# Keeping TensorE's instructions of the first layer in written order behind the opening as well

## The chip, the cores and the metric

The kernel runs on one core of one Trainium2 chip. The metric is the device time of one execution in microseconds, from launch to the last output, as the median of three runs. A profile of one further execution gives the times of the single instructions. Five engines matter: TensorE (PE, matrix products, with its own weight loads PEld), VectorE (DVE), ScalarE (ACT), GpSimd (POOL), and SyncE (SP), which here only issues DMA transfers. Each engine takes its instructions strictly in the order in which they stand in its own stream; a semaphore holds an instruction until the work that it reads is done, and everything behind it on that engine is held too.

## What is computed

A retention layer (attention with a fixed decay and no softmax) over 4 batches, 8 heads, 576 positions and head size 64, and behind it two feed-forward layers over the 2304 tokens, 512 wide with a hidden width of 2048:

```python
scores = scale * np.matmul(q, k.transpose(0, 1, 3, 2))
Dmat = np.where(rel >= 0, gamma[:, None, None] ** rel[None, :, :], 0.0)
x = np.matmul(scores * Dmat[None], v)         # then (B*S, H*D)
h = x @ w_in;  g = h * np.cos(h);  y = g @ w_out            # first layer
h = y @ w_in;  g = where(h >= 1, h, where(h <= -1, 0, (h + 1) ** 2 / 4));  out = g @ w_out   # second layer
```

Inputs and weights are given in float32 (the feed-forward weights in a wider form that the kernel converts itself).

## The kernel before

Every operand of a matrix product is split in a high and a low part, and a product is made of three: high by high, low by high and high by low.

**The first layer** runs in slots. The tokens are cut in five blocks (256, then four of 512), the hidden width in 16 pieces; a slot is one piece of one block, 80 in all. Slots 0 to 31 interleave blocks 0 and 1, slots 32 to 47 are block 2, 48 to 63 block 3, 64 to 79 block 4. In a slot, TensorE makes the *first product* (`mm1`, 12 matmuls into a PSUM bank `h`, line 599). Then follows a chain over three engines: a rounded copy on ACT (`turns`, 647), the remainder on DVE (`rounded`, 651), sine and square on ACT (655, 656), times h on DVE (660), the high part `gh` on ACT (667) and the low part `gl` on POOL (672). In blocks 0 and 1 ACT first copies h out of PSUM (`hs`, 642). TensorE's *second product* (`mm2`, 12 matmuls, lines 614 to 616) reads `gh`, `gl` and a piece of `w_out` and adds into four PSUM banks `bky` (two, `bkS` and `bkO`, for the 256-wide block). It is written two slots behind its first product: the text of slot s issues `mm1(s)`, then the rest of the chain of s-1, then `mm2(s-2)`.

**Retention** of the tokens of block 3 is done while block 2's slots run, that of block 4 while block 3's run: nine chunks of up to 128 tokens, here numbered 1 to 9 (1 to 5 belong to block 3). A chunk visits TensorE twice with small 64-row matmuls into the banks `bkS` and `bkO` (line 372). The *scores* visit (`scores`, `across`) comes first. DVE then multiplies both banks by a mask into the tile `R` (`masked`, two instructions on line 460), and the *attend* visit (`attend`, `state`) reads `R`. ACT and DVE then empty the banks into the next block's input (500, 507) and DVE updates a running state `T` (406). Before the chunk POOL scales its q and k (358, 368). The places of these steps are written as half slots: scores at g, attend a third of the way to the chunk's end e.

Beside this, DVE and ACT convert weights in the background (lines 196 to 277), and **the second layer**, from about 459 us on, runs with a scheme of seven products (`hq`, `wq`).

**What sets the order.** All engines' instructions are written in one program text. A scheduler then orders each engine's stream by its own estimate of when things are ready, except where the text pins them. The variable `by_hand` says what is pinned, through a wrapper `Ordered` around each engine; a pinned instruction is kept behind whatever stands before it on its engine. The opening (up to slot 7 or so) is listed by hand and pinned on all engines (`by_hand` 1). Behind it (`by_hand` 2) instructions only stay behind the opening's last one. From slot 24 on nothing is pinned (`by_hand` 0), and in the second layer TensorE alone is pinned (`by_hand` 3). Pinned instructions show line 107, the wrapper's, in place of their own. Line numbers are the same in both kernels. `keep_in_program_order` adds no wait: it fixes only which instruction stands behind which.

Of the kernel before, what the change touches and what calls it, by code (L numbers as in the profile page):

```python
# [89 lines left out]
def retention_moe_kernel(ctx: ExitStack, tc: tile.TileContext, qk, kv, win1, wout1, win2, wout2, rtab, ktab, out):  # L90
    nc = tc.nc
    by_hand = [0]
# [68 lines left out]
    def load_raw(L, i, c, late=False, homes=None):  # L161
        src = wsrc[L, i][c]
        twice = L == 0 and (i, c) not in ONCE
        tag = "raw" if twice else ("raw", "rsh")[turn[0] % 2] if L == 0 else ("raw", "raw", "rsh")[turn[0] % 3]
        turn[0] += not twice and not late
        pool, first, second = (wp, "wo0", None) if late else (cv, tag, "rsh") if homes is None else (wp, *homes)
        t = pool.tile([P, DM, 2], I32, tag=first, name="raw")
        i0 = SY.dma_start(out=t, in_=src)
        if L == 1 and len(done) > 1 and not late:
            behind(i0, done[-2])  # L170
        t2 = None
        if twice:
            t2 = pool.tile([P, 4 * DM], I16, tag=second, name="rsh")
            SY.dma_start(out=t2[:, 1:], in_=src.rearrange("p n two -> p (n two)").bitcast(I16)[:, :4 * DM - 1])
        raws[L, i, c] = t, t2
# [49 lines left out]
    def begin(L, i, c, after=None, late=False):  # L225
        return Conversion(L, i, c, after, late).X()
# [3 lines left out]
    def home1(i, c):  # L230
        if i == 0:
            wi[0, c] = wr.tile([P, 2, DM], F32R, tag="wi", name="wi")
            return wi[0, c]
        wo[0, c] = wp.tile([P, 2, DM], F32R, tag=f"wo{c}", name=f"wo{c}")
        return wo[0, c]

    def store1(c):
        SY.dma_start(out=wd[0, 0, c], in_=f(wi[0, c]))
# [42 lines left out]
    def load_wi(c):  # L281
        t = wr.tile([P, 2, DM], F32R, tag="wi", name="wi")
        SY.dma_start(out=f(t), in_=wd[0, 0, c])
        wi[0, c] = t
# [339 lines left out]
    def evac(s):  # L624
        l, c = slots[s]
        if c != NC - 1:
            return
        o, n = BLOCKS[l]
        per = 512 // n
        for e, y in enumerate(yb.pop(l)):  # L630
            t = stp.tile([P, 512], F32, tag="st", name="st")
            copy_out(e, t, y, -TWOPI)
            SY.dma_start(out=yd[:, e * per:(e + 1) * per, o:o + n], in_=t.rearrange("p (k n) -> p k n", k=per))
# [50 lines left out]
    def steps_of(s, which):  # L684
        for x in which:
            if (x, s) not in taken:
                taken.add((x, s))
                STEPS[x](s)
# [124 lines left out]
    def run_plan(pos):  # L813
        for fn in plan.pop(pos, []):
            fn()
# [173 lines left out]
    def spill_2(i, c):  # L989
        (spill_wi2, spill_wo2)[i](c, begun2.pop((i, c)))  # L990
        if i == 0 and c >= NQ:
            spill_sums(c - NQ)
# [12 lines left out]
    def run_pre(t):  # L1005
        for fn in pre.pop(t, []):
            fn()

    for s in range(N1):
        l, c = slots[s]  # L1010
        if s == 24:
            by_hand[0] = 0
        run_plan(2 * s)
        steps_of(s, "m")
        if s >= 1:
            steps_of(s - 1, "CgG")
        steps_of(s, "haA")

        todo = [x for x in jobs.get(s, []) if x not in opened]
        begun = [begin(0, *x) for x in todo]  # L1020
        for x in todo:
            begun.pop(0).rest(home1(*x))
            if x[0] == 0:
                store1(x[1])
            if queue:
                load_raw(0, *queue.pop(0))
        run_plan(2 * s + 1)
        if s >= LAG:
            steps_of(s - LAG, "M")
            evac(s - LAG)  # L1030
        for x in bgpos.get(s - 2, []):
            spill_2(*x)
        for x in bgpos.get(s, []):
            load_raw(1, *x)
        steps_of(s, "b")
        for x in bgpos.get(s - 1, []):
            begun2[x] = begin(1, *x, after=mark[0])
        for c2 in reload.get(s, []):
            load_wi(c2)

        q = 2 * (s - N1)
        if q >= -22:
            run_pre(q)
            run_pre(q + 1)
# [119 lines left out]
```

## Time and profile before

| | |
|---|---|
| median of 3 runs | 848.73 us (847.38 to 849.69) |
| the profiled execution | 848.21 us |
| its span, first to last instruction | 846.4 us |
| granted TensorE clock over the span | 0.999 of 2.4 GHz |
| PE busy | 835.2 us, 99% of the span |
| DVE, ACT, POOL busy | 576.6, 445.6, 142.2 us |

The span is what the trace covers; 1.8 us of the execution lie around it. A matmul's duration holds its pipeline: a 512-wide one is shown with 389 ns, while the next one starts 227 ns behind it. So a PE that is shown busy can still have been held for a tenth of a microsecond or so, and distances are best read from start to start.

### The profile page before, as it was taken

The numbers are of one execution on the slowest core, as the hardware profiler recorded it, in microseconds if no ns is written. First come the engines' busy times: TensorE is split into PE (matmuls) and PEld (weight loads), VectorE is DVE, ScalarE is ACT, GpSimd is POOL, SyncE is SP. The second block draws the span as 40 slices with busy tenths as digits, with TensorE's granted clock in tenths as the row PEclk, the third lists the DMA queues.
The fourth block names the chain that finished last, engine by engine and source line by source line (L and its number), as shares of the span: only waits on it lengthen the run. The fifth ranks groups of instructions, "written<-read, shape, count | busy, mean of one in ns | idle before, by whom it ended". The sixth has DMA issues, their size and how long they took to land.

```text
span 846.4 us, 14195 instructions
## 1 busy us (share of the span) xinstructions
PE 835.2 (99%) x5279; PEld 717.2 (85%) x5283; DVE 576.6 (68%) x1080; ACT 445.6 (53%) x868; POOL 142.2 (17%) x116
## 2 busy tenths in 40 slices
PE   8999999999999999999999999999999999999998
PEld 5778888888778888888888988989898898898986
DVE  7877888549776889677883676766554766554554
ACT  4877878755555655556665443344333344333333
POOL 3422322432324242222223000000000000000000
PEclk9999999999999999999999999999999999999999
DMA  9987999846868778678867877865755756755532
GB/s 351 407 323 266 340 328 328 308 139 217 286 217 307 275 286 275 228 256 310 298 237 239 276 254 231 273 195 174 258 190 169 275 177 178 261 183 175 160 88 75
DMA packets 68245, 207.72 MB, mean 245 GB/s; under 512 B 7376, under 2 KB 11216, under 8 KB 68176
## 3 DMA queue, kind: packets, MB, share of 16 engines
q1 hardware_dynamic: 68176, 206.81, 71.4%
q8 instruction: 42, 0.69, 0.3%
q14 instruction: 27, 0.22, 0.1%
HBM read 165.89 MB, written 40.89 MB: 244 GB/s over the span
## 4 chain that ended last, share of the span: by engine, by line
PE 86%; DMA 6%; DVE 4%; ACT 2%; issue 1%; SPq 0%; ACTq 0%; DVEq 0%
PE hq L107 20%; PE bky L107 17%; PE h L599 15%; PE bky L614 6%; PE bky L615 6%; PE bky L616 6%; PE bkO L107 4%; PE bkS L107 4%; DMA qkv<-in_kv_dram 2%; PE h L107 2%; PE bkS L372 1%; PE bkO L599 1%; PE bkS L599 1%; PE bkO L372 1%; DVE t L107 1%; DMA rsh<-in_wout_dram 1%
## 5 line engine op out<-in xcount | busy, mean ns | idle before, releaser
L107 PE MATMUL hq<-xc,wq 128*128 128x384 f32 x1008 | 202.8, 336 | 0.0
L107 PEld LDWEIGHTS hq<-xc,wq 128*128 128x128 f32 x1008 | 180.7, 188 | 15.0
L599 PE MATMUL h<-xhl,wi 128*128 128x512 f32 (+1 forms) x576 | 138.7, 388 | 0.0
L599 PEld LDWEIGHTS h<-xhl,wi 128*128 128x128 f32 x576 | 105.8, 188 | 22.6 <-issue 0.7
L107 PE MATMUL bky<-wo,gh 128*128 128x512 f32 x384 | 119.5, 392 | 0.0
L672 POOL TENSOR_TENSOR gl<-t,gh 128x512 fp32r<-128x512 f32 (+1 forms) x57 | 78.1, 1370 | 197.7 <-ACT gh L667 146.2
L781 ACT ACTIVATE t<-t,half 128x384 f32<-128x384 f32 x96 | 58.7, 612 | 86.2 <-DVE t L780 86.1
L614 PE MATMUL bky<-gh,wo 128*128 128x512 f32 x208 | 81.7, 393 | 0.0
L677 ACT ACTIVATE gh<-t 128x384 fp32r<-128x384 f32 x96 | 50.3, 525 | 59.3 <-DVE t L782 59.3
L615 PE MATMUL bky<-gh,wo 128*128 128x512 f32 x208 | 81.1, 390 | 0.0
L616 PE MATMUL bky<-gl,wo 128*128 128x512 f32 x208 | 78.7, 389 | 0.0
L107 PEld LDWEIGHTS bky<-wo,gh 128*128 128x128 f32 x384 | 70.4, 188 | 7.1
L107 PE MATMUL bky<-wo,gl 128*128 128x512 f32 x192 | 76.3, 397 | 0.0
L782 DVE TENSOR_TENSOR t<-t,sC 128x384 f32<-128x384 f32 x96 | 53.3, 555 | 18.9 <-ACT t L781 18.7
L678 DVE TENSOR_TENSOR gl<-t,gh 128x384 fp32r<-128x384 f32 x96 | 53.2, 554 | 18.1 <-ACT gh L677 17.8
L780 DVE TENSOR_SCALAR t<-sC 128x384 f32<-128x384 f32 x96 | 34.3, 358 | 43.4 <-ACT sC L767 41.7
L667 ACT ACTIVATE gh<-t 128x512 fp32r<-128x512 f32 (+1 forms) x57 | 35.3, 619 | 44.1 <-DVE t L660 44.1
L655 ACT ACTIVATE t<-t 128x512 f32<-128x512 f32 (+1 forms) x56 | 35.0, 624 | 40.2 <-DVE t L651 40.1
L107 PE MATMUL h<-xhl,wi 128*128 128x256 f32 (+1 forms) x288 | 52.0, 330 | 0.0
L107 PEld LDWEIGHTS h<-xhl,wi 128*128 128x128 f32 x288 | 43.6, 190 | 5.7 <-issue 0.5
L651 DVE SCALAR_TENSOR_TENSOR t<-t,h 128x512 f32<-128x512 f32 x40 | 27.4, 684 | 30.3 <-ACT t L647 29.8
L767 ACT ACTIVATE sC<-hq 128x384 f32<-128x384 f32 x24 | 11.8, 490 | 67.1 <-PE hq L107 67.1
(188 smaller groups left out, 1480.8 us busy)
## 6 DMA issues: line engine op xcount, KB each, us to landing
wq<-wq SPq DMA_DIRECT2D x72, 512.0 KB, 3.9
wi<-wd SPq DMA_DIRECT2D x48, 512.0 KB, 4.9
wo<-wd SPq DMA_DIRECT2D x48, 512.0 KB, 3.8
raw<-in_win_dram SPq DMA_DIRECT2D x32, 512.0 KB, 6.3
raw<-in_wout_dram SPq DMA_DIRECT2D x32, 512.0 KB, 5.7
qkv<-in_qk_dram SPq DMA_DIRECT2D x16, 512.0 KB, 6.1
qkv<-in_kv_dram SPq DMA_DIRECT2D x16, 512.0 KB, 7.0
wd<-wi SPq DMA_DIRECT2D x16, 512.0 KB, 6.1
```

Source lines behind the costliest of these rows:

```text
L107: ins = fn(*args, **kw)
L599: lastpe[0] = PE.matmul(hp[s][:, :n], w[:, a, kb, :], x[b][:, kb, :], start=(i == 0), stop=(i == 3 * KB - 1))
L614: PE.matmul(o, w[:, 0, es], a, start=first and e % per == 0, stop=False, skip_group_check=True)
L615: PE.matmul(o, w[:, 1, es], a, start=False, stop=False, skip_group_check=True)
L616: PE.matmul(o, w[:, 0, es], b, start=False, stop=last, skip_group_check=True)
L655: A.activation(u, u, AF.Sin, scale=TWOPI / 2)
L667: A.activation(gh[s], rt[s], AF.Copy)
L672: G.tensor_tensor(out=gl[s], in0=u, in1=f(gh[s]), op=ALU.subtract)
L677: A.activation(a, u, AF.Copy)
L678: V.tensor_tensor(out=b, in0=u, in1=f(a), op=ALU.subtract)
L781: A.activation(t, t, AF.Square, scale=0.5, bias=half)
L782: V.tensor_tensor(out=t, in0=t, in1=h, op=ALU.max)
```

## The change

One number: from slot 24 to the end of the first layer, `by_hand` is 3 where it was 0, so TensorE's stream there keeps the order of the text. The other engines stay free; the scheduler orders them anew around the pinned TensorE.

```diff
     for s in range(N1):
         l, c = slots[s]
         if s == 24:
-            by_hand[0] = 0
+            by_hand[0] = 3
         run_plan(2 * s)
         steps_of(s, "m")
```

Up to slot 23 all streams are the same. TensorE, at slot 24, before: `h` is a first product, `bky` a second product, and `wo_1611` the weights of the second product of slot 21, `wo_1820` those of slot 20.

```order
L107 MATMUL bkO<-gl,wo_1820 128x256
L107 MATMUL h<-xhl,wi 128x256 x8
L599 MATMUL h<-xhl,wi 128x512 x12
L107 MATMUL bky_1009<-gh,wo_1611 128x512 x2
L107 MATMUL bky_1010<-gh,wo_1611 128x512 x2
```

And now:

```order
L107 MATMUL bkO<-gl,wo_1820 128x256
L107 MATMUL h<-xhl,wi 128x256 x8
L107 MATMUL bky_1009<-gh,wo_1611 128x512 x2
L107 MATMUL bky_1010<-gh,wo_1611 128x512 x2
L107 MATMUL bky_1011<-gh,wo_1611 128x512 x2
L107 MATMUL bky_1012<-gh,wo_1611 128x512 x2
L107 MATMUL bky_1009<-gl,wo_1611 128x512
L107 MATMUL bky_1010<-gl,wo_1611 128x512
L107 MATMUL bky_1011<-gl,wo_1611 128x512
L107 MATMUL bky_1012<-gl,wo_1611 128x512
L107 MATMUL h<-xhl,wi 128x512 x12
```

The first product of slot 24 (the row with 12 matmuls of 512) stood ahead of slot 21's second product and stands behind it now.

TensorE, at the sixth chunk, before: the end of block 2's last second product (`wo_2161`, slot 47), then the start of the attend visit, which reads `R`.

```order
L614 MATMUL bky_2528<-gh,wo_2161 128x512
L615 MATMUL bky_2528<-gh,wo_2161 128x512
L616 MATMUL bky_2528<-gl,wo_2161 128x512
L599 MATMUL h<-xhl,wi 128x512 x5
L372 MATMUL bkS<-R,qkv 64x128
L372 MATMUL bkO<-R,qkv 64x128
```

And now, from the end of the scores visit (`qkv,T`) to the attend visit:

```order
L107 MATMUL bkO<-qkv,T 64x128
L107 MATMUL bkS<-qkv,T 64x128
L107 MATMUL h<-xhl,wi 128x512 x12
L107 MATMUL bkS<-R,qkv 64x128
L107 MATMUL bkO<-R,qkv 64x128
```

Between the scores and the attend visit stood the first product of slot 49, the second of slot 47 and 5 matmuls of the next first product; now the first product of slot 49 alone stands there. Chunks 1, 2, 3, 4, 5 and 8 likewise have one product block between the two visits now, chunks 7 and 9 two. The scores visit of chunk 6 was cut in two before, with 2 of its matmuls ahead of the first product of slot 46, and is whole now.

DVE, behind the second chunk, before: `T` is its state update, `xhl` its low part, `t` the chains of the slots (651 is `rounded`, 660 times h), and `cw`, `W`, `X`, `C` the conversions.

```order
L209 TENSOR_SCALAR W<-X 128x512
L210 TENSOR_SCALAR X<-W 128x512
L406 SCALAR_TENSOR_TENSOR T<-T,ktb,bkS 128x64 x2
L406 SCALAR_TENSOR_TENSOR T<-T,ktb,bkO 128x64 x2
L216 SCALAR_TENSOR_TENSOR cw<-C,X 128x512
L660 SCALAR_TENSOR_TENSOR t<-t,h 128x512
L507 TENSOR_TENSOR xhl<-bkS,xhl 128x2x128
```

And now:

```order
L406 SCALAR_TENSOR_TENSOR T<-T,ktb,bkS 128x64 x2
L406 SCALAR_TENSOR_TENSOR T<-T,ktb,bkO 128x64 x2
L277 TENSOR_TENSOR tw<-V,tw 128x4x256
L507 TENSOR_TENSOR xhl<-bkS,xhl 128x2x128
L507 TENSOR_TENSOR xhl<-bkO,xhl 128x2x128
L204 TENSOR_SCALAR C<-raw 128x512
L205 SCALAR_TENSOR_TENSOR C<-raw,C 128x512
L651 SCALAR_TENSOR_TENSOR t<-t,h 128x512
L209 TENSOR_SCALAR W<-X 128x512
L210 TENSOR_SCALAR X<-W 128x512
L216 SCALAR_TENSOR_TENSOR cw<-C,X 128x512
L660 SCALAR_TENSOR_TENSOR t<-t,h 128x512
```

The state update, the low part and a conversion step moved ahead of slot 36's `rounded`.

## Rows read from the trace of the kernel before

**Rows 1.** Stretches of the span: us, busy time of each engine, PEclk, DMA share, GB/s.

```profile
160.00:350.00 190.00, 190.00 (x1586) 153.70 (x1585) 139.79 (x246) 109.77 (x200) 61.94 (x47) 1.00 0.72 250
...
459.00:834.00 375.00, 374.56 (x1862) 336.04 (x1861) 224.50 (x451) 145.46 (x267) 1.29 (x1) 1.00 0.63 202
```

**Rows 2.** Timeline of PE at slot 24: start us, us, engine, line, operation, tiles.

```profile
133.90 1.12 PE L107 MATMUL h<-xhl,wi 128*128 128x256 f32 x8
134.99 3.02 PE L599 MATMUL h<-xhl,wi 128*128 128x512 f32 x12
137.85 1.98 PE L107 MATMUL bky<-gh,wo 128*128 128x512 f32 x8
...
140.92 0.28 PE L614 MATMUL bkS<-gh,wo 128*128 128x256 f32 x1
...
142.36 1.24 PE L599 MATMUL h<-xhl,wi 128*128 128x256 f32 x9
```

**Rows 3.** Timeline of ACT and of POOL there, slots 21 and 24.

```profile
135.91 0.62 ACT L107 ACTIVATE gh<-t 128x512 fp32r<-128x512 f32 x1
141.06 0.59 ACT L642 ACTIVATE hs<-h 128x512 f32<-128x512 f32 x1
136.66 1.30 POOL L107 TENSOR_TENSOR gl<-t,gh 128x512 fp32r<-128x512 f32 x1 [4.25 <-ACT gh L107]
147.41 1.31 POOL L672 TENSOR_TENSOR gl<-t,gh 128x512 fp32r<-128x512 f32 x1 [4.38 <-ACT gh L667]
```

**Rows 4.** Timeline of PE around the sixth chunk.

```profile
268.19 2.88 PE L599 MATMUL h<-xhl,wi 128*128 128x512 f32 x12
270.91 0.39 PE L614 MATMUL bky<-gh,wo 128*128 128x512 f32 x1
...
283.06 0.39 PE L614 MATMUL bky<-gh,wo 128*128 128x512 f32 x1
```

**Rows 5.** Timeline of DVE before the sixth chunk's attend visit.

```profile
271.80 0.69 DVE L651 SCALAR_TENSOR_TENSOR t<-t,h 128x512 f32<-128x512 f32 x1 [2.70 <-ACT t L647]
272.41 1.31 DVE L209 TENSOR_SCALAR W<-X 128x512 int32<-128x512 int32 x1
...
281.20 0.41 DVE L209 TENSOR_SCALAR W<-X 128x512 int32<-128x512 int32 x1
...
284.79 0.55 DVE L460 TENSOR_TENSOR R<-bkS,mtb 128x384 f32<-128x384 f32 x1
```

**Rows 6.** Timeline of POOL in the same stretch.

```profile
272.13 1.30 POOL L358 TENSOR_TENSOR qkv<-qkv,qtb 128x512 f32<-128x512 f32 x1 [0.95 <-DMA qkv<-in_qk_dram]
```

**Rows 7.** Timelines of DVE and PE at the eighth chunk.

```profile
324.89 0.54 DVE L460 TENSOR_TENSOR R<-bkS,mtb 128x384 f32<-128x384 f32 x1
324.50 2.88 PE L599 MATMUL h<-xhl,wi 128*128 128x512 f32 x12
```

**Rows 8.** Timelines of DVE and PE at the second and the third chunk.

```profile
192.06 1.16 DVE L209 TENSOR_SCALAR W<-X 128x512 int32<-128x512 int32 x1
200.22 0.55 DVE L460 TENSOR_TENSOR R<-bkS,mtb 128x384 f32<-128x384 f32 x1
200.00 2.88 PE L599 MATMUL h<-xhl,wi 128*128 128x512 f32 x12
215.71 0.55 DVE L460 TENSOR_TENSOR R<-bkS,mtb 128x384 f32<-128x384 f32 x1
216.65 0.39 PE L614 MATMUL bky<-gh,wo 128*128 128x512 f32 x1
```

**Rows 9.** Groups of DVE, 165 to 350 us: shapes, count | busy us, mean ns | idle before.

```profile
L507 DVE TENSOR_TENSOR xhl<-bkS,xhl 128x256 fp32r<-128x256 f32 (+1 forms) x8 | 3.1, 391 | 5.2 <-ACT xhl L500 5.0
...
L406 DVE SCALAR_TENSOR_TENSOR T<-T,ktb,bkS 128x64 f32<-128x64 f32 x12 | 2.8, 276 | 0.5 <-PE bkS L372 0.5
```

**Rows 10.** Timelines of DVE and PE at the first chunk.

```profile
181.10 0.55 DVE L460 TENSOR_TENSOR R<-bkS,mtb 128x384 f32<-128x384 f32 x1
183.37 0.39 PE L614 MATMUL bky<-gh,wo 128*128 128x512 f32 x1
```

## The prediction

> **What bounds the kernel now.** I read the busy time by stretches first. In the main part of the stretch that the change reaches, TensorE is busy without a gap (190.00 of 190 us), at a granted clock of 1.00, the upper level of 2.4 GHz [rows 1]. Since a matmul's row also covers its pipeline, that alone proves little. So I went to TensorE's timeline and read from start to start: a product block of twelve 512-wide matmuls takes 270.91 - 268.19 = 2.72 us [rows 4], which is 227 ns a matmul, and a first product behind narrower matmuls 137.85 - 134.99 = 2.86 us [rows 2]. Blocks follow each other at these prices through all of slots 24 to 79. The first layer behind the opening is therefore bound by TensorE's issue, and the order of before already hides every chain on the other engines. Of the second layer's stretch 374.56 of 375 us are busy too [rows 1].
>
> From this follows the form of the sum. The change neither adds nor removes a matmul, so the blocks cost the same in any order. Little can be won. What can be lost is a place where the written order asks for an operand earlier than its engine delivers it: TensorE then stands still, and since it is the bound, all of that goes on the end. So I looked, place by place, for what the new order asks for and when the trace of before had it. All times are put on the clock of the trace of before.
>
> **Slot 24.** Slot 21's second product now follows directly on the matmuls of 133.90, that is at 134.99 [rows 2]. Its high part `gh` is made by ACT from 135.91 to 136.53 [rows 3]. All streams are the same up to there, so nothing makes it earlier. Before, the first product of slot 24 filled that time. TensorE stands still 136.53 - 134.99 = 1.54, with some 0.06 for the signal **1.6 us**. The low part ends at 137.96 and is wanted behind eight matmuls, at 138.4: no second wait.
>
> **Slot 24's own chain.** The 256-wide blocks around it are short (142.36 - 140.92 = 1.44 us [rows 2]), so the written distance of two slots is short here. The first product of slot 24 now ends at 136.6 + 2.72 + 2.86 = 142.2. Behind it come the second product of 22, first of 25, second of 23 (1.44 each) and the first of 26 (2.86): its own second product starts at 149.4, and its third matmul, the first with `gl`, at 149.8. The chain in before, from ACT's copy to the end of POOL's `gl`, ran from 141.06 to 148.72, 7.7 us [rows 3]. Now ACT can start the copy at 142.7 or so, behind a conversion, so `gl` comes at 150.4 to 150.6: a wait of **0.8 us**. From below it is 0 (a chain shorter by 0.8, since ACT and DVE are put in another order there), from above 1.5 (a second conversion in front of the copy).
>
> **Chunks.** The attend visit waits for DVE's second mask instruction. In before a scores visit was followed by two blocks or more; now often by one. So I compare the end of that instruction with the time at which the first block behind the scores visit ended.
> - Chunk 1: ready at 181.65, wanted at 183.37 [rows 10]. No wait, 1.7 us to spare. Chunks 4 and 5 have 64 columns, shorter masks, and no wait either; 7 and 9 keep two blocks.
> - Chunk 2: ready at 200.77, wanted at 200.00 [rows 8], a wait of 0.8 as it stands. But the DVE queue in front of it was late because a conversion step took 1.16 us [rows 8], while the same step takes 0.41 undisturbed [rows 5], with POOL scaling the next chunk's q and k beside it. That next chunk's load waits until the first chunk's attend visit has freed its buffer; that visit now comes one block sooner, so the scaling should be over before the conversion. I take **0.2**, between 0 and 0.85.
> - Chunk 3: ready at 216.26, wanted at 216.65 [rows 8], 0.4 to spare. But DVE now does the state update, the low part and a conversion step ahead of slot 36's `rounded`. Of the six instructions, the four of the update take some 0.23 each (2.8 us for 12) and the two of the low part some 0.39 [rows 9], 1.7 us together; ACT's part of slot 37 stands behind the late slot 36. I take **0.3**, between 0 and 1.2.
> - Chunk 6: ready at 285.34 [rows 5], wanted at 283.06 [rows 4], a wait of **2.3 us**. DVE is busy from 271.80 to there without a break, and what starts it is slot 47's first product, which stands at the same distance as before: from 270.91 to 283.06 stand three blocks, the scores visit and one more block in either order. From below 0.7 (rivals), from above 2.8.
> - Chunk 8: ready at 325.43, wanted at 324.50 [rows 7]. **0.9**, between 0.2 and 1.1.
>
> At chunk 6 the trace shows a conversion step of 1.31 us, begun at 272.41, where the same step took 0.41 at 281.20 [rows 5], and POOL scaling a chunk from 272.13 to 273.43 [rows 6]. The Trainium skill (SBUF — State Buffer, Who interferes with whom) says that DVE's faster mode and GpSimd share a pair of ports under a lock, and that the later one is held until the first has finished. By that rule the step was held until 273.43 and then took its 0.41, so it should have lasted 1.4 us; the trace agrees with 1.31. By that rule the wait at chunk 6 goes down where POOL's scaling no longer falls on these steps; that is the first rival.
>
> **What is given back.** The scores visit of chunk 6 is whole again. A product block behind narrower matmuls costs 2.86 in place of 2.72 [rows 2, 4], 0.14 more; the turn into the narrow ones I put at about as much, so one turn in and out less gives **-0.3 us**, between -0.6 and 0. The second layer is as bound by TensorE as the first [rows 1] and its order is unchanged, so the waits are not made up there.
>
> **Sum:** 1.6 + 0.8 + 0.2 + 0.3 + 2.3 + 0.9 - 0.3 = 5.8 us. The profiled execution took 848.21 (span 846.4 and 1.8 around it), so 854.0. The median of the runs is 0.5 above the profiled execution and within their spread of 2.3; I predict **854.0 us**, slower by 0.7%.
>
> **Rivals.**
> 1. *The DVE backlog dissolves.* With the two waits of slot 24 and earlier attend visits, transfers, and so POOL's scaling, fall on other DVE instructions. At chunk 6 the conversion step would then take 0.41 in place of 1.31, 0.9 less; I put what the steps behind it lose to the rest of the scaling at another 0.7, so the wait falls to 0.7. At chunk 8 it falls to 0.2, chunks 2 and 3 have none. For it: loads are tied to the attend visits. Against it: chunk 7's load, whose scaling falls on chunk 6's backlog, hangs on TensorE's slots as much as on the fifth chunk. Sum 1.6 + 0.8 + 0.7 + 0.2 - 0.3 = 3.0, so 851.2: still slower, by 0.35%.
> 2. *Not slower: the reordered ACT and DVE deliver in time.* The scheduler knows the pinned order and has reordered the other engines for it. If slot 24's own chain and all masks come in time, only the wait for slot 21's `gh` is left, since the streams in front of it are the same: 1.6 - 0.3 = +1.3, 849.5, within 0.3%. It decides from the point on which the masks come one block behind the scores. For it: the mask of chunk 1 had 1.7 us to spare. Against it: DVE's order around the masks of chunks 6 and 8 is unchanged.
> 3. *Late chains feed each other.* Every place at its upper bound: 1.6 + 1.5 + 0.85 + 1.2 + 2.8 + 1.1 = 9.1, 857.3. For it: DVE has little slack (139.79 busy of 190 [rows 1]), and ACT, DVE and POOL also hold later slots back. Against it: a still TensorE gives the others time to catch up.
> 4. *The change does nothing.* Excluded: the streams differ at the places shown.
>
> **How the numbers follow.** The forecast 0.50, rival 1 0.20, rival 2 0.13, rival 3 0.13, and 0.04 for a gain that I don't see, at most the few tenths of the turns between wide and narrow. A measurement of this kernel can tell about 0.3%, 2.5 us. Slower by more than that are the forecast, rival 3, and most of rival 1: 0.80. Within it are rival 2 and the rest of rival 1: 0.17. Faster: 0.03. The range runs from rival 2's 849.5 to 858.5, rival 3 with a microsecond for waits in block 4's slots that I haven't priced; the forecast's own range is 852 to 856.
>
> **What would show it.** In the new profile TensorE should stand still at about 135 us, waiting for ACT's `gh`, for some 1.5 us; at about 151 for POOL's `gl`; and before the attend visits of chunks 6 and 8, waiting for DVE's `R` (about 285 and 330 us). PE's idle time between 134 and 350 us should add up to 5 to 6 us, or a little less where the pipeline hides its first tenths. Blocks between the waits should still take 2.72 us and the second layer its 375. Wrong is the working if a wait of over a microsecond stands at a place not named, if the second layer's length changes, if the granted clock falls behind a wait, or if the masks of chunks 6 and 8 are ready in time.

## The result and the profile after

The changed kernel takes 854.62 us (median of 6 runs, 853.95 to 856.33), the kernel before 848.39 beside it: a ratio of 1.0077 (95% interval 1.0064 to 1.0090), slower, with 854.0 predicted. Timed a second time (the ninth experiment) the ratio was 1.0065 (1.0051 to 1.0079).

The waits of TensorE in the new profile, from 130 us to the second layer (engine, tile, line <- what it waited for: us in total, times, longest). The same view of before had no line.

```profile
PE bkS L107 <- DVE R L460: 2.6, 2, 1.8
PE bky L107 <- POOL gl L672: 1.0, 2, 0.6
PE bky L107 <- ACT gh L107: 0.9, 1, 0.9
```

The stretches that answer to [rows 1] (us, busy time of each engine, PEclk, DMA share, GB/s), before and behind the first layer's end:

```profile
134.00:160.00 26.00, 24.53 (x144) 21.34 (x143) 19.52 (x35) 20.78 (x45) 6.84 (x7) 1.00 0.87 316
160.00:350.00 190.00, 187.38 (x1543) 152.00 (x1542) 135.55 (x245) 108.73 (x196) 60.13 (x47) 1.00 0.71 245
...
465.00:840.00 375.00, 374.55 (x1861) 335.63 (x1860) 224.25 (x451) 144.77 (x267) 1.30 (x1) 1.00 0.62 202
```

TensorE, busy without a gap before, now has holes of 1.47 and 2.62 us, 4.1 together (5.6 in the second profile), where 5 to 6 was predicted; the clock is 1.00 in them and behind them. In 375 us of the second layer TensorE is busy for as long as before.

**Slot 24** [rows 2, 3]. TensorE, ACT's high part of slot 21, and POOL's low part of slot 24, in that order (start, duration, operation, and in brackets the idle time before it and what ended it):

```profile
135.12 1.12 PE L107 MATMUL h<-xhl,wi 128*128 128x256 f32 x8
137.13 2.14 PE L107 MATMUL bky<-gh,wo 128*128 128x512 f32 x8 [0.89 <-ACT gh L107]
...
149.80 0.62 PE L107 MATMUL bky<-gh,wo 128*128 128x512 f32 x2
151.01 0.50 PE L107 MATMUL bky<-gl,wo 128*128 128x512 f32 x1 [0.58 <-POOL gl L672]
...
136.46 0.61 ACT L107 ACTIVATE gh<-t 128x512 fp32r<-128x512 f32 x1
...
149.67 1.28 POOL L672 TENSOR_TENSOR gl<-t,gh 128x512 fp32r<-128x512 f32 x1 [6.75 <-ACT gh L667]
```

Slot 21's second product starts 2.01 us behind the eight narrow matmuls, which last 0.96 undisturbed (in the second experiment): 1.05 lost. Slot 24's second product runs from 149.80 to 153.40, 3.60 in place of 2.72: 0.88 lost. Both waits are the predicted ones. The first is shorter than 1.6 here because this execution's opening was late; of that below.

**Chunk 6** [rows 4 to 6]. TensorE behind the scores visit, DVE up to the masks, and POOL:

```profile
282.49 3.02 PE L107 MATMUL h<-xhl,wi 128*128 128x512 f32 x12
287.27 0.32 PE L107 MATMUL bkS<-R,qkv 64*64 64x128 f32 x1 [1.77 <-DVE R L460]
...
276.80 1.19 DVE L251 TENSOR_TENSOR V<-W,X 128x512 f32<-128x512 f32 x1
278.03 1.15 DVE L270 TENSOR_TENSOR V<-V 128x256 f32<-128x256 f32 x1
279.10 1.51 DVE L263 TENSOR_TENSOR cw<-V,cw 128x256 fp32r<-128x256 f32 x1
...
286.20 0.55 DVE L460 TENSOR_TENSOR R<-bkO,mtb 128x384 f32<-128x384 f32 x1
286.67 0.55 DVE L460 TENSOR_TENSOR R<-bkS,mtb 128x384 f32<-128x384 f32 x1
...
275.99 1.46 POOL L358 TENSOR_TENSOR qkv<-qkv,qtb 128x512 f32<-128x512 f32 x1 [2.04 <-DMA qkv<-in_qk_dram]
277.65 1.24 POOL L368 TENSOR_TENSOR qkv<-qkv,ktb 128x512 f32<-128x512 f32 x1 [0.21 <-DMA qkv<-in_kv_dram]
278.86 1.48 POOL L672 TENSOR_TENSOR gl<-t,gh 128x512 fp32r<-128x512 f32 x1
```

One product block stands between scores and attend, 4.78 us long in place of 2.86: 1.92 lost. The masks are ready at 287.22. In front of them three conversion steps last 1.19, 1.15 and 1.51 while POOL works on chunk 7 and a low part.

**Chunk 8** [rows 7], from the second product behind the scores visit to the attend visit:

```profile
325.74 0.73 PE L107 MATMUL bky<-gh,wo 128*128 128x512 f32 x2
...
329.61 0.32 PE L107 MATMUL bkS<-R,qkv 64*64 64x128 f32 x1 [0.85 <-DVE R L460]
```

The block takes 3.87 us. A second product behind narrow matmuls takes 2.85 to 2.88 undisturbed (behind chunk 6's attend visit, in the two profiles of the change), so 1.0 is lost to DVE's `R`.

**Slot 75**, in block 4, was not named in the prediction. First TensorE and POOL after, then the same before:

```profile
448.06 2.88 PE L107 MATMUL bkS<-xhl,wi 128*128 128x512 f32 x12
450.78 0.61 PE L107 MATMUL bky<-gh,wo 128*128 128x512 f32 x2
451.78 0.50 PE L107 MATMUL bky<-gl,wo 128*128 128x512 f32 x1 [0.38 <-POOL gl L672]
...
450.44 1.29 POOL L672 TENSOR_TENSOR gl<-t,gh 128x512 fp32r<-128x512 f32 x1 [5.13 <-ACT gh L667]
```

```profile
445.79 1.07 PE L599 MATMUL h<-xhl,wi 128*128 128x512 f32 x4
446.70 0.39 PE L614 MATMUL bky<-gh,wo 128*128 128x512 f32 x1
...
448.06 0.84 PE L616 MATMUL bky<-gl,wo 128*128 128x512 f32 x3
...
445.43 1.29 POOL L672 TENSOR_TENSOR gl<-t,gh 128x512 fp32r<-128x512 f32 x1 [5.13 <-ACT gh L667]
```

Before, the scheduler had put four matmuls of the next first product and six of `gh` ahead of the first that needs `gl`. In written order `gl` is wanted third and comes too late, which costs 0.7 us.

**Where the time went.** Each stage below ends where the same amount of matmul work is left before the second layer, so the columns compare the same work; two executions of each kernel.

| stage, us | before | before, again | after | after, again |
|---|---|---|---|---|
| start of the eight narrow matmuls at slot 24 | 133.90 | 132.53 | 135.12 | 133.00 |
| from there to about slot 30's second product | 42.97 | 42.98 | 44.63 | 46.90 |
| chunks 1 to 5 | 83.92 | 83.92 | 83.91 | 83.91 |
| up to chunk 6's scores visit | 15.56 | 15.56 | 14.96 | 14.96 |
| chunk 6 | 15.72 | 15.72 | 17.55 | 17.56 |
| chunks 7, 8 | 41.67 | 41.70 | 42.56 | 42.11 |
| chunk 9, slots to 74 | 107.75 | 107.74 | 107.75 | 107.75 |
| slot 75 | 6.12 | 6.12 | 6.79 | 6.92 |
| to the second layer | 11.78 | 11.79 | 11.81 | 11.81 |
| from the narrow matmuls to the second layer | 325.49 | 325.53 | 329.96 | 331.92 |

In these rows the kernel before repeats to 0.05 us; the change costs 4.5 us in its first profile and 6.4 in the second. The second layer, behind the last row, does not repeat as well: from its first matmul to the end of the span it takes 387.0 and 387.5 us before, 387.4 and 386.4 after. TensorE waits there once for DVE's `gl`, 0.4 to 0.5 us in three of these profiles and not in the fourth. This differs by execution and not by kernel, and the rows leave it out.

**The opening** ends at another time in each execution. In the change's first profile TensorE stood still for 2.1 us at 56 us (for a mask that stands in DVE's queue behind a conversion, whose transfer DVE had waited 5.0 us for), and behind it the granted clock fell (stretches as above):

```profile
56.00:58.00 2.00, 0.00 (x0) 0.00 (x0) 1.66 (x4) 0.58 (x3) 0.00 (x0) 1.00 1.01 399
58.00:60.00 2.00, 1.98 (x17) 1.57 (x18) 1.93 (x6) 1.84 (x6) 0.73 (x1) 0.67 1.02 414
60.00:62.00 2.00, 2.00 (x6) 1.60 (x5) 2.00 (x5) 1.31 (x4) 0.08 (x1) 0.50 0.54 221
62.00:64.00 2.00, 2.00 (x10) 1.57 (x10) 1.97 (x6) 1.97 (x5) 0.00 (x0) 0.98 0.03 12
```

0.50 is the lower level, 1.2 GHz. All instructions up to there are the same in every kernel of this study, so this isn't the change's doing. The table starts behind the opening, because its end (the table's first row) differs by up to 2.6 us between these four profiles.

### The profile page after: what moved, and what is told of

Its sections match the earlier page's. It is cut to its first block, busy times and chain, and to the rows that moved or that the text cites. A ratio compares the mean times of both kernels' runs of the same rounds, so it can differ in the third digit from the quotient of the medians.

```text
span 852.5 us, 14188 instructions
## 1 busy us (share of the span) xinstructions
PE 835.9 (98%) x5279; PEld 717.7 (84%) x5283; DVE 574.1 (67%) x1080; ACT 446.9 (52%) x868; POOL 139.4 (16%) x116
## 4 chain that ended last, share of the span: by engine, by line
PE 69%; DVE 9%; DMA 2%; ACT 2%; issue 1%; SPq 0%; ACTq 0%; DVEq 0%
PE bky L107 27%; PE hq L107 20%; PE h L107 12%; PE bkS L107 5%; PE bkO L107 5%; DVE cw L263 1%; DVE t L651 1%; DVE xc L730 1%; DMA rsh<-in_wout_dram 1%; DMA q<-yd 1%; DMA wq<-cw 1%; DVE t L660 1%; DVE X L250 1%; DVE W L209 0%; DVE V L251 0%
## 5 line engine op out<-in xcount | busy, mean ns | idle before, releaser
L107 PE MATMUL h<-xhl,wi 128*128 128x512 f32 (+1 forms) x864 | 190.4, 369 | 0.0
L107 PE MATMUL bky<-gh,wo 128*128 128x512 f32 x512 | 156.6, 392 | 0.9 <-ACT gh L107 0.9
L107 PEld LDWEIGHTS bky<-gh,wo 128*128 128x128 f32 x512 | 94.9, 188 | 20.9 <-ACT gh L107 1.1
L107 PE MATMUL bky<-gl,wo 128*128 128x512 f32 x256 | 97.4, 391 | 1.0 <-POOL gl L672 1.0
L107 PEld LDWEIGHTS bky<-gl,wo 128*128 128x128 f32 x256 | 47.9, 188 | 11.8 <-POOL gl L672 1.8
L755 DVE TENSOR_TENSOR sC<-hq,sW 128x384 f32<-128x384 f32 x48 | 26.5, 553 | 25.2 <-PE hq L107 25.1
```

Of the source, the lines that this page charges most:

```text
L107: ins = fn(*args, **kw)
L755: V.tensor_tensor(out=t, in0=hq[which][:, :TH], in1=a, op=ALU.add)
```

## The experiments

"Inner length" is the last row of the table above (325.5 before), read from the experiment's own profile; the ratio is of its runs to runs of the kernel before on the same chip. 0.001 of the ratio is 0.85 us.

**1. Pinned in slots 24 to 31 alone.**

```diff
             by_hand[0] = 3
+        if s == 32:
+            by_hand[0] = 0
```

> TensorE pinned in written order for slots 24 to 31 alone and left free from slot 32 on, as before the change. Theory (each wait of TensorE that the new trace shows is lost for good, place by place): only the two waits around slot 24 are left, for slot 21's high part (block of 8 narrow matmuls 2.01 us long in place of about 0.95, so 1.1) and for slot 24's low part (0.9). 848.4 + 2.0 = 850.4 us; no wait before the attend visits of chunks 6 and 8, none at slot 75. Rival 1 (the loss comes from the pinned later slots' knock-on, and the waits at slot 24 are made up where the scheduler is free again): 848.4 to 849. Rival 2 (the opening of the changed kernel is what is slower, its clock dip of 1.3 us in the profile being systematic): 849.7 or more even without the waits, and 851.7 with them.

Measured: 1.0035 (1.0022 to 1.0048), about +3.0 us; inner length 328.04, +2.6. Its waits from 134 us to the second layer:

```profile
PE bky L107 <- ACT gh L107: 1.5, 1, 1.5
PE bky L107 <- POOL gl L672: 0.7, 1, 0.7
```

Only slots 21 and 24 are left, and nothing is made up later. Start to start they cost 1.69 (2.65 for the narrow block) and 1.04 (3.76 for slot 24's second product), more than the change's first profile showed: the opening was 1.2 us earlier here, and the operands were not earlier by as much. The excess over 2.0 is this, and not a slower opening, so rival 2 falls with rival 1.

**2. Pinned from slot 32 on.**

```diff
-            by_hand[0] = 3
+            by_hand[0] = 0
+        if s == 32:
+            by_hand[0] = 3
```

> TensorE free for slots 24 to 31 and pinned in written order from slot 32 on. Theory: the two waits around slot 24 go (2.0 us), the waits before the attend visits of chunks 6 (1.9) and 8 (1.0) and at slot 75 (0.7) stay: 854.6 - 2.0 = 852.6 us. Additivity: what this kernel and the one pinned for slots 24 to 31 lose against the kernel before adds up to the change's 6.2. Rival 1 (TensorE's waits at slot 24 gave the other engines time, so without them the masks are later still): 853.5 to 854.6, with chunk 6's wait over 2.5. Rival 2 (a part of the loss is the opening's clock): shows as a granted clock under 1.00 before 134 us.

Measured: 1.0034 (1.0020 to 1.0048), +2.9 us; inner length 328.33, +2.8; waits for `R` 2.5 us in two, for slot 75's `gl` 0.6. Less than the 4.2 expected against the kernel before, because I had not counted the 0.6 that is given back, and had put the opening's share of the change's 6.2 on the waits. Experiments 1 and 2 add up to 5.9 us, between the 6.5 and 5.5 that the change measured: within that, what the two groups of places cost adds up. This profile's own opening was the worst, with a still of 2.9 us and the clock at 0.50 from 58 to 64 us; its granted clock falls there and nowhere behind 134 us.

**3. The attend visit one block later.**

```diff
-            pos = [g, g + (e - g) // 3, e]
+            pos = [g, g + max(2, (e - g) // 3), e]
```

> Pinned as in the change, with the attend visits of chunks 1 to 6 and 8 written one half slot later, so that two product blocks stand between scores and attend in place of one. Theory: the mask of chunk 6 is ready at 287.2 in the new trace and is then wanted at 288.1, that of chunk 8 at 329.6 and wanted at 331.3, so both waits go (1.9 and 1.0): 854.6 - 2.9 = 851.7 us; the waits around slot 24 and at slot 75 stay. Rival 1 (the later attend frees the chunk's buffer later, so loads and POOL's scaling fall on other DVE work and new waits come up of a microsecond each): 853 to 855. Rival 2 (the loss is not in these waits): 854.6.

Measured: 1.0043 (1.0028 to 1.0058), +3.6 us, 2 to 3 under the change; inner length 328.78. The stages of chunk 6 (15.73) and of chunks 7 and 8 (41.67) are back at the length of before to 0.01 us: one block more between the two visits removes both waits. But a new one of 1.0 us stands at slot 29. POOL's low parts of slots 29 and 30 (the sixth experiment's expectation counts them as 30 and 31) are queued behind a scaling of k that waits for its transfer, and TensorE comes for slot 29's as written. Rival 1 had its mechanism right, at another place. That it hangs on the transfer and not on the later attend, which comes behind it, the ninth experiment shows.

**4. Slot 24's first product ahead of slot 21's second.**

```diff
         steps_of(s, "m")
+        if s == 24:
+            steps_of(21, "M")
...
-        if s >= LAG:
+        if s >= LAG and s != 23:
             steps_of(s - LAG, "M")
```

> Pinned as in the change, but the text of slot 21's second product moved behind slot 24's first product, the order that the kernel before has at this place. Theory: the wait for slot 21's high part goes (1.1), and because slot 24's first product then ends 3.8 us sooner while its second product starts only 1.1 sooner, the wait for slot 24's low part goes too (0.9): 854.6 - 2.0 = 852.6 us, all later waits as in the change. Rival 1 (the low part of slot 24 is held by ACT's and DVE's order, not by its first product): only 1.1 goes, 853.5. Rival 2 (what is saved is lost again at chunk 6, whose mask DVE finishes at a time of its own): 854.6.

Measured: 1.0052 (1.0036 to 1.0068), +4.4 us; inner length 328.82. The wait for slot 21's `gh` is gone; of slot 24's, 0.67 is left (its second product takes 3.39). TensorE behind slot 24's first product and at its second, then ACT's copy for slot 24:

```profile
138.39 0.61 PE L107 MATMUL bky<-gh,wo 128*128 128x512 f32 x2
...
148.33 0.61 PE L107 MATMUL bky<-gh,wo 128*128 128x512 f32 x2
149.30 0.50 PE L107 MATMUL bky<-gl,wo 128*128 128x512 f32 x1 [0.35 <-POOL gl L672]
...
141.61 0.58 ACT L642 ACTIVATE hs<-h 128x512 f32<-128x512 f32 x1
```

From the end of slot 24's first product to its second there are 9.9 us now (138.39 to 148.33), 7.1 in the change (142.74 to 149.80), but ACT took up slot 24's copy 3.2 us after it was ready (138.39 to 141.61). So rival 1 is right here: with the first product earlier, the order of ACT sets that wait. In the change itself the copy started 0.6 us behind the first product's end (143.31), with one conversion in between, so there the place of the first product set it too.

**5. POOL's scaling of chunk 7 later.**

```diff
-            gl_ = max(g - 9, ends.get(i - 2, -99))
+            gl_ = max(g - (5 if g == 104 else 9), ends.get(i - 2, -99))
```

> Pinned as in the change; only the load of chunk 7's q and k is written four half slots later, so POOL scales them behind two more low parts. DVE's order is the same as in the change, instruction for instruction. In the change's trace the three conversion steps in front of chunk 6's masks last 1.19, 1.15 and 1.51 us (lines 251, 270, 263) while POOL scales chunk 7; elsewhere they last 0.68, 0.43 and 0.41. Theory (chunk 6's wait is the written order plus 2.3 us that POOL's scaling costs DVE): these steps fall to about 0.7, 0.45 and up to 1.5 (the low part on POOL may still meet the last one), the masks come 1.2 to 2.3 us sooner, the wait falls from 1.8 to 0.6 or 0, and the time is 1.2 to 1.8 us under the change's; about 5 us over the kernel before in place of 6.5. Rival (DVE's backlog is its own, its length set by the chains): the wait stays at 1.8, the time at the change's. Rival 2 (the scaling, moved, falls on other masks): chunk 7 or 8 waits instead, same time.

DVE's three steps, the last mask, and TensorE at chunk 6:

```profile
277.42 0.69 DVE L251 TENSOR_TENSOR V<-W,X 128x512 f32<-128x512 f32 x1
278.14 0.43 DVE L270 TENSOR_TENSOR V<-V 128x256 f32<-128x256 f32 x1
278.59 1.40 DVE L263 TENSOR_TENSOR cw<-V,cw 128x256 fp32r<-128x256 f32 x1
...
286.05 0.55 DVE L460 TENSOR_TENSOR R<-bkS,mtb 128x384 f32<-128x384 f32 x1
...
283.10 3.02 PE L107 MATMUL h<-xhl,wi 128*128 128x512 f32 x12
286.66 0.32 PE L107 MATMUL bkS<-R,qkv 64*64 64x128 f32 x1 [0.54 <-DVE R L460]
```

Two of the steps are back at 0.69 and 0.43; the third still meets a low part on POOL. The wait falls from 1.92 to 3.56 - 2.86 = 0.70 us. POOL's scaling beside DVE thus made 1.2 of chunk 6's wait, and DVE's queue the rest. Rival 2 is right in small: chunk 7's attend visit, with two blocks in front, comes 5.85 us behind its scores visit here and 5.67 in the change, 0.2 lost. The whole time hides this: 1.0054 (1.0040 to 1.0067), +4.6 us, lies between the change's two ratios less 1.2, and the inner length is 330.72, because in this execution slot 29's wait of 1.0 stands as well.

**6. Pinned in slots 32 to 63, with the later attend.** Experiments 2 and 3 together, and free again at slot 64.

```diff
-            by_hand[0] = 3
+            by_hand[0] = 0
+        if s in (32, 64):
+            by_hand[0] = 3 * (s == 32)
```

> TensorE pinned in slots 32 to 63 alone, and the attend visits of chunks 1 to 6 and 8 one half slot later; slots 24 to 31 and block 4 are left free. Theory: all places that waited are gone (slots 21 and 24 and slot 75 are free, chunks 6 and 8 have two blocks in between) and what is given back at chunk 6's scores visit (0.6 us in every pinned kernel so far) stays: 0.6 us under the kernel before, no wait of TensorE in the first layer behind 134 us. Rival 1 (POOL's low parts of slots 30 and 31, queued behind a scaling that waits for its transfer, hold TensorE as in the kernel with only the later attend): 0.4 us over the kernel before. Rival 2 (pinning itself costs, beyond the waits): 2 us or more over it.

Measured: 0.9993 (0.9983 to 1.0004); inner length 324.90, -0.6. TensorE has no wait from 132 us to the second layer:

```profile
160.00:350.00 190.00, 190.00 (x1589) 154.07 (x1588) 139.98 (x248) 109.66 (x200) 59.57 (x47) 1.00 0.73 252
```

**7. The second product three slots behind the first, with the later attend** of experiment 3, pinned from slot 24 to the end.

```diff
-        if s >= LAG:
-            steps_of(s - LAG, "M")
-            evac(s - LAG)
+        if s != 23 and s >= LAG:
+            d = s - (LAG if s < 23 else LAG + 1)
+            steps_of(d, "M")
+            evac(d)
...
-    rest = [N1 - 2, N1 - 1]
+    rest = [N1 - 3, N1 - 2, N1 - 1]
```

> TensorE pinned in written order from slot 24 as in the change, but the second product is written three slots behind the first from slot 23 on (slot 21's now behind slot 24's first product), and the attend visits of chunks 1 to 6 and 8 come one half slot later. Theory (the change loses only because the written distances are too short): no wait at slots 21, 24 and 75 and none before an attend visit; 0.6 us under the kernel before. Rival 1 (the longer distance keeps gh and gl buffers longer, so the chains of later slots are held and new waits come): a wait of TensorE for gl in each block, 2 to 5 us over the kernel before. Rival 2 (pinning itself costs): as the change, 6 us over.

Measured: 0.9992 (0.9983 to 1.0001); no wait of TensorE behind the opening. Its second layer begins one second product earlier, so 2.72 is added to its inner length: 321.78 + 2.72 = 324.50, -1.0. Pinning costs nothing by itself; the written distances did. That the two kernels (6 and 7) beat the one before is read from the traces alone, up to the second layer: the intervals of both ratios hold 1.

**8. The same with the attend where the change has it.**

> As the kernel with the second product three slots behind the first, but with the attend visits where the change has them. Theory: the waits around slot 24 and at slot 75 go (2.4 and 0.7 us), those of chunks 6 and 8 stay (1.8 and 0.9), 0.6 is given back: 2.1 us over the kernel before. Rival 1 (chunk 6's mask is late because second products stand where they stand, so another distance moves it): chunk 6's wait under 1.0, 1 us over. Rival 2 (the waits at slot 24 come back at another place): 4 us or more over.

Measured: 1.0039 (1.0025 to 1.0053), +3.3 us; inner length 325.76 + 2.72 = 328.48, +3.0. Waits, and TensorE at chunk 3:

```profile
PE bkS L107 <- DVE R L460: 3.8, 3, 2.2
...
211.79 3.02 PE L107 MATMUL h<-xhl,wi 128*128 128x512 f32 x12
215.42 0.32 PE L107 MATMUL bkS<-R,qkv 64*64 64x128 f32 x1 [0.60 <-DVE R L460]
```

The waits for `gh` and `gl` are gone, those for `R` grew: 2.2 at chunk 6, 1.0 at chunk 8, 0.6 at chunk 3 (215.42), which waits in no other kernel. The longer distance is no remedy for the masks. Between experiments 7 and 8 only the attend visits differ, by 4.0 us of inner length.

**9. The change again.**

> The changed kernel itself, timed and profiled once more. In its first profile the stretch from the end of slot 23's first product to the second layer is 4.5 us longer than before, while the runs differ by 6.5 (1.0077); that execution's opening was 1.2 us late, with the granted clock at 0.50 from 60 to 62 us, and the wait for slot 21's high part was 1.1 where the other kernels with this wait show 1.7. Theory (the opening differs by execution, not by kernel; the change costs 2.4 around slot 24, 1.8 + 0.9 at chunks 6 and 8, 0.7 at slot 75, less 0.6 given back): 5.2 us over the kernel before, 1.0061, with clocks of 0.997 to 1.00 as every other kernel has. Rival (the changed kernel's opening is slower each time): 6.5 us again, clocks of 0.997 to 0.998 in all runs, and the block of slot 23 starting at 135 us or later.

Measured: 853.08, ratio 1.0065 (1.0051 to 1.0079), so about 5.5 us; mean granted clocks of 0.999 to 1.000 in its runs. The opening is not slower each time: the rival falls. But the inner length was 331.92, +6.4, and not 5.2; behind that, the second layer was 0.7 to 1.2 us shorter in this execution than in the two of the kernel before, which brings the profile near the runs' 5.5. TensorE at slots 21 and 29, then POOL at slot 29:

```profile
133.00 1.12 PE L107 MATMUL h<-xhl,wi 128*128 128x256 f32 x8
135.67 2.11 PE L107 MATMUL bky<-gh,wo 128*128 128x512 f32 x8 [1.54 <-ACT gh L107]
...
172.76 0.61 PE L107 MATMUL bky<-gh,wo 128*128 128x512 f32 x2
174.53 0.50 PE L107 MATMUL bky<-gl,wo 128*128 128x512 f32 x1 [1.15 <-POOL gl L672]
...
172.21 1.05 POOL L368 TENSOR_TENSOR qkv<-qkv,ktb 128x512 f32<-128x512 f32 x1 [2.46 <-DMA qkv<-in_kv_dram]
173.22 2.97 POOL L672 TENSOR_TENSOR gl<-t,gh 128x512 fp32r<-128x512 f32 x2
```

In the change's first profile the same scaling started at 171.85 and TensorE was at 174.08 there, so nothing waited. Here the transfer came at about the same time, but TensorE was 1.3 us earlier: 4.19 in place of 2.72, 1.5 lost. The two executions began the narrow matmuls 2.1 us apart (135.12 and 133.00) and reached the end of the next stage 0.15 apart (179.75 and 179.90). So in these two executions the earlier opening gained the pinned kernel nothing: 0.65 more was lost at slot 21, 0.18 at slot 24 and 1.5 at slot 29. It is no rule: in experiment 3, with waits at the same three places, the narrow matmuls began 2.66 us earlier than in the change's first profile (132.46), and chunk 1's scores visit was still 1.0 earlier (181.35 against 182.34).

**10. The kernel before again.**

> The kernel before, one more profile. Theory (the opening's end varies between executions of the same instructions, the rest doesn't): slot 23's block starts anywhere between 132 and 137 us, and from there to the second layer's first matmul it takes 325.5 us within 0.3, as in the first profile, without a wait of TensorE. Rival (the rest varies too): another length by over 1 us.

Measured: the narrow matmuls start at 132.53, the inner length is 325.53, no wait. The rival falls.

## Why the prediction was right

The total, the sign and the mechanism held: TensorE was the bound, the places where the written order asks too early became stalls (chunks 2 and 3 excepted, which were in time), and none was made up.

| term, us | predicted | first profile | second profile |
|---|---|---|---|
| slot 21's `gh` | 1.6 | 1.05 | 1.70 |
| slot 24's `gl` | 0.8 | 0.88 | 1.06 |
| slot 29's `gl` | not named | 0 | 1.5 |
| chunks 2 and 3 | 0.5 | 0 | 0 |
| chunk 6 | 2.3 | 1.92 | 1.92 |
| chunk 8 | 0.9 | 1.0 | 0.5 |
| slot 75's `gl` | not named | 0.7 | 0.8 |
| given back (what is left over) | -0.3 | -1.1 | -1.1 |
| from slot 24 to the second layer | 5.8 | 4.5 | 6.4 |

- *Slot 24.* The size of the first wait was worked out for an opening like that of before; with one (133.96 in experiment 1) it is 1.69. The second came as worked out: the first product ended at 142.74, ACT's copy started 0.6 behind it, and the chain from there to the end of `gl` took 7.6 (143.31 to 150.95). Incomplete was the reason: experiment 4 shows that an earlier first product alone does not remove the wait, since ACT then takes the copy 3.2 us late.
- *Chunks 2 and 3.* Mis-sized: there was no wait. The masks were ready 0.8 and 0.5 us before they were wanted (202.19 and 202.98, 219.09 and 219.62); only with three slots' distance did chunk 3 lose 0.6.
- *Chunk 6.* Right place, 0.4 too much. POOL's scaling did fall on DVE's conversion steps again, as I held against the first rival, though on others: the step of line 209 took 0.42 this time, those of lines 251 and 270 were long. Experiment 5 takes the scaling away and leaves 0.70, the price that this rival gave for it. These steps are `tensor_tensor`, and what the prediction took from the Trainium skill (SBUF — State Buffer, Who interferes with whom), DVE's faster mode, is not theirs by the same section; it says of a DVE instruction with two inputs in SBUF that it contends with a GpSimd instruction that reads SBUF. The runs agree, with 1.19 and 1.15 us beside the scaling and 0.69 and 0.43 without.
- *Given back.* Chunk 6's scores visit, cut in two before, took 0.37 + 1.04 us, whole it takes 1.05, and a turn in and out of narrow matmuls (0.15 and 0.09) goes: 0.36 + 0.24 = 0.6. I had the turns alone. The other 0.5 is what the waits, summed start to start, exceed the stages by: 0.3 of it at slots 24 to 30, where the narrow block and the product behind it took 1.09 and 2.86 before [rows 2], 3.95 together, but 3.71 in experiment 8 and 3.92 in experiment 4, which have one order there. So 0.96 for the narrow block undisturbed holds for some executions only, and the waits at slot 21 are known to some 0.1. The last 0.2 lies at chunks 6 and 8, half each; its cause is open.
- *Not named.* Slot 75's 0.7 was in the range, as waits of block 4 that I hadn't priced. Slot 29's wait of 1.5 us in the second profile is, by my own words, a wait of over a microsecond at a place not named: the working was incomplete there. I had compared only the masks and the two waits at slot 24 with the trace of before, and missed that POOL's queue holds a low part behind a scaling that waits for a transfer.
- *The rivals.* The second (only slot 21's wait) fell with chunk 6's, and the upper bounds together were not reached.

The 854.0 so met 854.62 partly by luck: 0.5 for chunks that did not wait stood in for slots 29 and 75, and the first profile's other 1.2 us came from its opening. The first ratio's 6.5 us and the second's 5.5 have overlapping intervals; the runs of the first have mean granted clocks of 0.997 to 0.998, those of the second 0.999 to 1.000, as if the opening's clock had fallen in all six of the first; runs that were only timed have no trace, so that is argued and not shown. For it speaks that among 23 runs of the kernel before the five with a mean clock of 0.998 or less have a median of 848.6 us, the other eighteen one of 846.9.

## What to carry to other kernels

When the bound engine is to be kept in written order, compare for every operand on every queue when the written order wants it with when the old trace has it, transfers that an operand is queued behind included; a free order may be covering a late chain with four matmuls borrowed from the next product. The remedy for each wait is distance in the text, and it is specific: one slot more for the second products and one block more before the attend visits took all of them away, each only its own kind. Compare kernels over a stretch that repeats between executions (for the kernel before, from slot 24 to the second layer), and look at more than one profile of the changed kernel, whose waits may not repeat.

## What the runs showed of the hardware

Of the twelve profiles, four show the granted clock at 0.50 for some microseconds behind the still at 56 us: the change's first, and experiments 2, 7 and 8, after stills of 2.1, 2.9, 2.1 and 2.3 us. Experiments 4 and 5 had stills of 2.2 and 2.1 there and kept 1.00, and TensorE's stills in the first layer, up to 2.2 us at chunk 6 in experiment 8, were never followed by a lower clock. In those four the narrow matmuls of slot 24 start at 134.8 to 137.0 us, in the other eight at 132.5 to 134.5. The times of one kernel spread by some 3 us (845.9 to 849.1 in 23 runs of the kernel before). In the profiles the opening, with and without the lower clock, and the second layer (386.1 to 387.5 us from its first matmul to the end, in the ten profiles without the three slots' distance) vary, while the stretch between differs by 0.05 in the two profiles of the kernel before; how much of the spread each makes in the runs without a trace is not shown.
